# Inverse transform matrices from sines instead of TensorE turns, a new opening and a new order in a long-convolution and FFN kernel

## The chip, the cores and the metric

The kernel runs on one core of one Trainium2 chip. The metric is the device time of one execution in microseconds (us). The engines are called as in the profile: PE is TensorE (PEld its weight loads), DVE is VectorE, ACT is ScalarE, POOL is GpSimd, SP is the engine whose queue issues most DMAs.

## The reference

All tensors are bf16; S = 2048 rows, D = 640 columns, F = 1728. The input x is normalized, goes through a gated convolution (A) and through a two-layer FFN (B), and the two are multiplied and added to x.

```
xn = layernorm(x)
# A: shift filter of 4 taps on k, gate by v, causal convolution of length S per column, gate by xn
k_shift = sum over t of k[s - (3 - t)] * shift_k[:, 3 - t]
kv = k_shift * v
y = irfft(rfft(kv padded to 2S) * rfft(ssm_k padded to 2S))[:S] + kv * ssm_D
s = xn * y
# B
g = silu(gelu(xn @ w1 + b1) @ w2 + b2)
out = x + s * g
```

## The kernel before

The convolution is computed as a Fourier transform of 4096 points in two steps, written as matrix products. The rows are split as 128 partitions times NJ = 16. A first product (F1) takes the 16 groups of 128 rows through 128x128 matrices that hold cosines and sines, for the filter (steps `kf`, evictions `ke`) and for kv (`uf`, `ue`). The results go to DRAM (`ks`, `us`) and come back with the rows regrouped (`fl`, `ml`). A second product (F2, `ff` and `mu`) uses small 32x32 blocks. The two transforms are multiplied (`mp`, `mq` on DVE: the second factor has real and imaginary rows exchanged by the DMAs `mk`), a first inverse product follows (`ma`, `mb`, eviction `me`), a trip through DRAM again (`ms`, `yl`), and the second inverse product `y`. `yt` multiplies by the gate, `yo` adds x, `ys` stores. Each 1280-column pair of rows is cut into three tiles of 428, 426 and 426 columns, one PSUM bank each, so there are 48 tiles in each of these steps and 24 in `y`.

The FFN works on four chunks of 512 rows. `h` is a tile of the first product (14 per chunk: h0 to h13, h14 to h27, h28 to h41, h42 to h55), `he` its GELU on ACT, `g` a tile of the second product (8 per chunk, 14 matmuls of 320 columns each), `ge` its SiLU on ACT, `gm` the multiplication into xn on DVE. Layernorm of the chunks 1 to 3 is `ls` (statistics, DVE), `lv`, `lr` (the root, POOL), `ln` (normalization, DVE or ACT), `tt` and `te` (turn and eviction). `kt` and `kc` turn the filter. `cv` are the eight DVE steps of the shift filter for each of eight pairs of rows.

The cosine and sine matrices of F1 are WA and WB, 128 x 16 x 128 each. They are made once, from an integer product of row and column numbers (`build_f1_product`, `w`), by Sin and Abs on ACT (`ws`). The second inverse product needs the same matrices, each 128x128 block turned; GA and GB are the names for these, in the same memory. Before, 32 turns on PE (`it`, four steps of eight) and four DVE copies (`ie`) turn WA and WB in place once F1 is done with them.

Everything is issued in one hand-ordered list: after `prologue()` the string `PLAN` names step after step, and its letters behind a dot say which engine evicts (`.a` ACT, `.d` DVE). Each engine works through its own instructions in that order. PSUM banks and slots of the working area are handed out from lists in the order of the plan (`ones`, `slots`). `TURNS` says for each tile which rotation of the 32x32 blocks it uses. `use_table` keeps count of which set of functions ACT has loaded: GELU with one, SiLU with another, and Sin runs with the second.

The opening, `prologue()`, loads x, w1 and the parameters, runs warming products (`warm`, products of the identity whose result nobody reads), takes the four taps of the shift filter over the partitions (`tap`), normalizes chunk 0 in two halves (`bn`, `ag`, `sq`, `rc`, `norm_dve`), turns them (`turn`, `turned_out`) and does the first six FFN1 tiles in two halves (`first_block`). The bias b1 and the skip weight D arrive as rows (`prm`), are turned on PE into the bank `pt` and copied by DVE. `small_bits`, `small_first` and `small_second` prepare the small matrices of F2 and of the first inverse.

Of the kernel before, what the change touches and what calls it, by code (L numbers as in the profile page):

```python
# [10 lines left out]
F32 = mybir.dt.float32  # L11
BF16 = mybir.dt.bfloat16
I32 = mybir.dt.int32
ACT = mybir.ActivationFunctionType
# [14 lines left out]
WARM = (6, 3, 1)  # L29
NFIRST = 6  # L30

TURNS = "301213011202320033233310212313130220012202211303"

PLAN = """
em4 s h13 he1 em7 w he0 X1 ls5 K1 K0 he3 he5 he2 ls6 ls7 ls4 lv1 lr1 em6 em5 h12 h9 he13 he4 h10 ee7.a he12 ee6.a
ee5.a he9 ee4.a h11 cv8 cv16 cv17 ln5.d B1 B0 he10 h6 cv0 cv18 cv19 ln4.d h7 ln7.a he11 ln6.a h8 tt9 cv9 cv1 he6 B2
he7 tt8 tt5 C4 he8 ss g0 ws0 ge0 cv10 cv20 cv21 te8.d tt6 g2 g1 tt7 C0 C3 C1 cv22 cv11 cv2 te9.d te6.d cv12 sm C2
te7.d X2 d K3 V6 cv3 kt9 kc9.d kt7 ws1 te5.a ws2 kt5 V0 K2 ge1 kc7.a ge2 cv4 gm1.d V3 V1 V5 kc5.d kt3 kt13 kt14 kf28
kc14.a kt11 kt2 kt8 ke28.a kc3.d kc11.d V2 kc8.a kt10 kt12 kc13.d kc2.d kc10.d kt6 kf10 kt4 V4 kc12.a X3 V7 ke10.a
kf15 kf27 kc4.d kc6.d kf9 kt1 kc1.d kt15 ke27.a ke15.a kf31 kt0 kc15.d kc0.d ke9.a kf41 cv32 cv33 cv5 gm0.d ke31.a  # L40
kf16 kf39 kf17 ke16.a kf44 kf11 kf29 kf45 kf14 ke17.a ke11.a ke29.a ke44.a ke45.a ke39.a ke41.a ks9 ks3 g3 ge3 kf38
kf42 kf24 ke42.a cv34 ke14.d cv6 cv13 cv7 cv14 cv40 kf13 kf33 kf12 kf40 ke24.a kf0 ke33.a ke13.a gm3.d cv35 ke40.a kf3
ke12.a ke3.a g4 ke0.a gm2.d ge4 kf30 kf34 ke34.a kf46 kf37 kf35 ke30.a kf5 kf47 g5 ks4 ke46.a ke47.a ks13 cv36 cv37
ke38.a ke5.a ke37.a ks15 ke35.a kf36 ke36.a cv24 cv38 ks11 kf4 kf32 ke4.a kf6 kf1 kf21 kf43 ke21.a ke6.a ke32.a ge5
ke43.a g6 ks5 ks1 ks12 cv48 cv39 cv56 cv49 cv41 cv23 ge6 kf2 ke2.a cv57 cv42 cv43 gm4.d kf23 kf25 kf22 kf20 kf26
ke23.a ke22.a cv50 ke25.a g7 uf26 ke1.a cv51 cv15 ke20.a ke26.a ue26.a ks14 ks10 kf18 uf4 ue4.a kf19 ke19.a ke18.a
uf14 kf8 uf24 kf7 ue24.a h26 ks0 ks7 ks8 ks6 ue14.a ke8.a ke7.a ks2 ge7 gm7.d uf25 h15 uf12 ue25.a ue12.a uf13 ue13.a
he26 h20 h24 uf0 ue0.a he15 he24 uf27 uf8 h21 fl15 uf5 he20 he21 h19 he19 ue8.a uf9 uf17 ue17.a h22 he22 ue5.a ue9.a
uf16 uf28 ue27.a ue28.a ls8 cv44 cv45 cv52 cv46 gm6.d cv47 ls10 ue16.d cv25 h23 uf10 uf33 he23 h16 us8 uf29 ue33.a
ue29.a uf32 uf34 ue32.a uf15 uf35 h27 he16 ue35.a h18 he27 uf3 h25 he18 ue10.a us4 cv53 gm5.d ue3.a ue15.a he25 cv26  # L50
uf7 h17 he17 ls11 cv27 cv54 fl1 fl11 fl7 fl9 fl14 ls9 cv28 cv55 ue7.d lv2 cv29 cv58 us5 fl5 fl2 uf6 ue6.a ue34.a lr2
cv59 h14 uf40 uf1 uf2 uf11 uf38 uf30 fl4 fl3 he14 uf37 ue2.a ue11.a ue1.a g8 ue30.a ue38.a ge8 uf31 uf41 ln8.d cv60 g9
cv30 cv61 ue40.a ue41.a fl0 fl6 fl8 ue31.a cv31 uf22 uf39 uf23 ue22.a ue23.a uf21 uf19 uf36 ue21.a ue39.a ge9 ln9.d
cv62 ln10.d cv63 ue19.a ue37.a g10 uf18 ff10 ls12 ue36.d ln11.d fl12 ff46 ff13 ff8 ge10 ue18.a uf20 uf45 fe10.d uf42
uf44 uf43 us11 us2 us9 us0 us3 us10 us1 ue20.d fe8.a ue45.a ue44.a fe13.a ff15 ff7 ff19 uf46 ue42.d uf47 ue43.d fe46.a
tt13 fe19.d ff23 ff21 fe15.d ff6 ff3 ue46.a ue47.a fe7.a us13 us7 te13.d us12 fe21.d fe23.a ff2 us6 tt12 tt10 fe3.a
fe6.d it2 ff24 ff12 ff4 tt14 us14 te10.a fe2.a te12.d ie2.d te14.d it0 us15 fe12.a fe4.a fe24.a mk2 tt11 ff47 ff11
ff36 ie0.d te11.d fl10 it1 fe11.a fe36.a ls14 ie1.d gm8.d ff9 ff16 ff1 ff28 fe1.a fe28.a fe9.a ml2 g11 fe47.a fe16.a
ff29 ff38 ff44 ls15 fe38.d ge11 ff25 ff33 ff27 it3 fe44.a ml3 ff20 ff14 ff26 fe29.a fe27.a fe25.a fe26.a fe33.a fe14.a
ml0 ml4 mk3 ml1 ml8 g12 ff35 mu7 ff18 gm9.d ie3.d ls13 mu6 fe20.d gm11.d ff5 mu8 ff34 gm10.d lv3 ge12 g14 fe18.a  # L60
fe34.a mp7 mp8 mq8 mu9 ma7 lr3 fe35.a fe5.a mu10 mq7 ff43 mk4 ml7 mk1 ff42 fe42.a mb7 g13 mp6 mp9 mq6 mp10 mq10 ln15.a
fe43.a me7.a ge13 ff22 mu13 gm12.d mq9 ff0 ff17 mu11 fe0.a fe22.a ge14 fe17.a ln12.a mp11 mq11 g15 mu12 mp13 mq13
gm13.d ge15 mk8 mu24 ff30 h39 mp12 mq12 mp24 ff32 ff45 mu26 mu4 h28 fe30.a he39 fe45.a he28 fe32.a mp4 mp26 mq24 mq4
mq26 h29 mu5 mu14 he29 ma11 mb11 ff37 ff31 ma24 h30 fe37.a fe31.a mk6 me11.a ml6 fl13 mp5 mq5 ma5 ma9 mu25 ma10 mb24
mp14 mq14 he30 mb5 mp25 mq25 mu19 ml11 mb9 ml5 mb10 mk5 me24.a h40 mu18 ma6 ma8 me9.a mu2 me10.a me5.a he40 mp19 mq19
mb8 ff41 fe41.a me8.a h32 ma12 ma13 mu16 mb13 mk0 mp18 mb12 mp2 mq18 mp16 mq16 mb6 h34 mu3 he32 ma4 ff40 me13.a me6.a
me12.a mq2 mp3 mk7 he34 mu22 mb4 mu15 ff39 fe39.a mp15 mp22 h31 me4.a fe40.a he31 h36 ma14 q6 ml9 mq22 mq3 mq15 mu21
# [798 lines left out]
```

## Time and profile before

| | us |
|---|---|
| median of 3 runs | 200.44 |
| lowest and highest | 200.13, 200.51 |
| the profiled execution | 202.52 |
| its span, first to last instruction | 200.7 |
| granted clock, mean | 0.991 |

| engine | busy us | share |
|---|---|---|
| PE | 189.0 | 94% |
| DVE | 171.8 | 86% |
| ACT | 154.7 | 77% |
| POOL | 43.5 | 22% |

The profile is one execution; its busy times are the union of instruction durations, and durations of neighbours on one engine overlap a little. An "idle before" in brackets names the length of the wait and what ended it. The windows view gives, for a stretch of the span, the busy time of each engine, then the clock that TensorE was granted (1.00 is full), then the share of the DMA engines and their rate in GB/s.

### The profile page before, as it was taken

Reading aid. Unit: us, or ns where it says so; the run is one execution under the profiler, and the core shown is the slowest. Engines: PE = TensorE matmul, PEld = TensorE weight load, DVE = VectorE, ACT = ScalarE, POOL = GpSimd, SP = SyncE. Lnnn points to the kernel's source line nnn. Section 1 sums busy time; section 2 is a strip of 40 time slices with the busy share of each in tenths; the row PEclk is TensorE's granted clock in tenths of the full one; section 3 lists DMA queues with packets and bytes.
Section 4 is the critical chain, followed back from the end, with each engine's and each line's share of the span. In section 5 each row is a group of like instructions: output and inputs, shape, how many; then the busy total and the mean of one; then the engine's idle time right before and its main releaser. Section 6 shows DMA issues by size and latency. Waiting matters only on the chain.

```text
span 200.7 us, 5123 instructions
## 1 busy us (share of the span) xinstructions
PE 189.0 (94%) x1941; PEld 113.3 (56%) x1954; DVE 171.8 (86%) x366; ACT 154.7 (77%) x311; POOL 43.5 (22%) x77
## 2 busy tenths in 40 slices
PE   7699999799999999999999999997999999999990
PEld 2377467776665455656656334454665544677770
DVE  7769999999999999989999999999899500479991
ACT  3546999999999999999989999996877538801120
POOL 8100400003454003753020000113145500001230
PEclk9969999999999999999999999999999999999999
DMA  6999999983598899799899978989469869951164
GB/s 200 346 365 308 338 394 409 399 319 137 219 366 322 284 350 364 291 341 344 266 314 337 283 242 280 331 286 349 139 229 330 289 212 369 395 219 65 50 251 163
DMA packets 27057, 57.69 MB, mean 287 GB/s; under 512 B 3032, under 2 KB 15513, under 8 KB 27032
## 3 DMA queue, kind: packets, MB, share of 16 engines
q1 hardware_dynamic: 22528, 39.65, 57.4%
q0 software_dynamic: 4320, 17.70, 23.8%
q8 instruction: 15, 0.25, 0.5%
q14 instruction: 10, 0.08, 0.1%
q10 hardware_dynamic: 184, 0.01, 0.1%
HBM read 33.76 MB, written 18.35 MB: 260 GB/s over the span
## 4 chain that ended last, share of the span: by engine, by line
PE 52%; ACT 34%; DVE 5%; issue 3%; DMA 3%; POOL 1%; ACTq 1%; POOLq 0%
PE banks L486 22%; ACT area L145 19%; PE banks L460 13%; PE banks L409 6%; ACT hT L472 5%; DMA prm<-in_A_ssm_D_dram 3%; ACT sl L492 2%; PE banks L742 2%; PE banks L675 2%; PE banks L676 2%; DVE st L416 2%; PE banks L444 1%; ACT xn L435 1%; DVE area L630 1%; ACT WA L322 1%
## 5 line engine op out<-in xcount | busy, mean ns | idle before, releaser
L145 ACT CAST area<-banks 128x426 bf16<-128x426 f32 (+2 forms) x179 | 81.7, 639 | 3.9 <-PE banks L409 3.6
L486 PE MATMUL banks<-w_sb,hT 128*128 128x320 bf16 x448 | 65.6, 299 | 0.3
L460 PE MATMUL banks<-xnT,w_sb 128*128 128x512 bf16 x217 | 53.6, 379 | 0.7
L486 PEld LDWEIGHTS <-hT 128*128 128x128 bf16 x448 | 42.9, 98 | 20.0 <-issue 3.0
L630 DVE TENSOR_TENSOR area<-banks,area 128x426 bf16<-128x426 f32 (+1 forms) x96 | 50.4, 595 | 1.9 <-PE banks L409 1.1
L472 ACT ACTIVATE hT<-banks,b_f 128x512 bf16<-128x512 f32 x52 | 34.2, 705 | 7.0 <-PE banks L460 5.2
L460 PEld LDWEIGHTS <-w_sb 128*128 128x128 bf16 x230 | 21.4, 98 | 25.9 <-issue 3.9
L492 ACT ACTIVATE sl<-banks 128x320 bf16<-128x320 f32 x32 | 15.4, 493 | 20.6 <-PE banks L486 14.5
L570 DVE TENSOR_TENSOR area<-area 128x1280 bf16<-128x1280 bf16 x32 | 25.4, 818 | 0.3
L684 DVE TENSOR_TENSOR area<-banks,xn 128x426 bf16<-128x426 f32 (+1 forms) x18 | 10.0, 596 | 15.5 <-PE banks L676 15.5
L660 POOL DMA_DIRECT2D scrC<-area x16 | 11.7, 731 | 44.1 <-DVE area L630 25.0
L409 PE MATMUL banks<-area,mats 32*32 32x426 bf16 (+1 forms) x768 | 19.4, 345 | 0.1
L566 DVE TENSOR_TENSOR area<-area 128x1280 bf16<-128x1280 bf16 x24 | 19.3, 814 | 0.0
L526 PE MATMUL banks<-area,WB 128*128 128x214 bf16 (+1 forms) x64 | 15.6, 299 | 0.1
L526 PE MATMUL banks<-area,WA 128*128 128x212 bf16 (+1 forms) x64 | 15.3, 298 | 0.1
L541 POOL DMA_DIRECT2D scrK<-area x16 | 8.8, 554 | 30.2 <-ACT area L145 29.1
L409 PEld LDWEIGHTS <-mats 32*32 32x32 bf16 x768 | 8.0, 88 | 11.1 <-issue 8.6
L552 POOL DMA_DIRECT2D scrU<-area x16 | 8.7, 546 | 18.7 <-ACT area L145 17.2
L146 DVE CAST area<-banks 128x426 bf16<-128x426 f32 (+1 forms) x17 | 9.5, 590 | 1.7 <-ACT area L145 1.1
L498 DVE TENSOR_TENSOR xn<-xn,sl 128x320 bf16<-128x320 bf16 x32 | 9.9, 318 | 1.0 <-ACT sl L492 1.0
L416 DVE BATCH_NORM_STATS2 st<-xn 128x6 f32<-128x320 bf16 x24 | 10.4, 476 | 0.0
L693 POOL DMA_DIRECT2D out_dram<-area x6 | 3.3, 547 | 31.9 <-DVE area L689 26.4
(101 smaller groups left out, 194.6 us busy)
## 6 DMA issues: line engine op xcount, KB each, us to landing
scrK<-area POOLq DMA_DIRECT2D x16, 320.0 KB, 3.0
scrU<-area POOLq DMA_DIRECT2D x16, 320.0 KB, 3.6
area<-scrK SPq DMA_DIRECT2D x16, 320.0 KB, 7.1
area<-area SPq DMA_DIRECT2D x32, 160.0 KB, 3.6
area<-scrU SPq DMA_DIRECT2D x16, 320.0 KB, 5.3
scrC<-area POOLq DMA_DIRECT2D x16, 320.0 KB, 4.0
area<-scrC SPq DMA_DIRECT2D x16, 320.0 KB, 6.5
area<-in_A_k_dram SPq DMA_DIRECT2D x4, 640.0 KB, 9.4
```

What stands on the lines that cost most here:

```text
L145: return nc.scalar.copy(out=out_ap, in_=in_ap)
L409: nc.tensor.matmul(out=out[b, :], lhsT=mats[a, m, a], rhs=rhs[a, :], start=start, stop=stop)
L416: nc.vector.bn_stats(out=st[:, j, h, :], in_=xn_tiles[c][:, j, h * HALF:(h + 1) * HALF])
L460: nc.tensor.matmul(out=ps, lhsT=w1_sb[:, t, ft * P:(ft + 1) * P], rhs=xnT[:, t, :], start=(t == 0), stop=(t == DT - 1))
L472: nc.scalar.activation(out=hT[:, ft, :], in_=one(("h", i)), func=ACT.Gelu_apprx_tanh, bias=b1_f[:, ft:ft + 1], scale=1.0)
L486: nc.tensor.matmul(out=ps[:, 0:HALF], lhsT=hT[0:M, ft, q * P:(q + 1) * P], rhs=w2_sb[0:M, ft, hs], start=(ft == 0), stop=(ft == FT - 1))
L492: nc.scalar.activation(out=sl[:], in_=one(("g", i))[:, 0:HALF], func=ACT.Silu)
L526: nc.tensor.matmul(out=ps[:, dst], lhsT=(WA, WB)[r][:, n2, :], rhs=rows[:, n2 % 2, src], start=True, stop=True)
L566: nc.vector.tensor_tensor(out=uc, in0=uc, in1=tmp, op=ALU.add)
L570: nc.vector.tensor_tensor(out=tmp if s else uc, in0=kh[:, r0:r0 + KC, :], in1=w_exp[:, j:j + 1, :].to_broadcast([P, KC, D]), op=ALU.mult)
L630: nc.vector.tensor_tensor(out=flat(("p", i))[:, x * w:x * w + w], in0=one(("mu", i))[:, 0:w], in1=flat(key)[:, cols(j)], op=ALU.mult)
L660: nc.gpsimd.dma_start(out=pair_view(scrC)[g2], in_=pair(("c", g2)))
```

## The change

Three parts of the code change, and with them the whole order.

The inverse matrices are computed directly. `ir` makes on POOL two short integer vectors per partition; for each quarter i of 4 x 128 columns, `ip` makes on DVE the integer product that stands in the turned matrix, `ia` takes it modulo L, `is` makes the sine on ACT into GB, `ib` the absolute value, and `ic` the cosine into GA. The integers lie in a slot of the working area. `it` and `ie` are gone. In the new order quarter 1 stands around the last products of the filter and kv, and the quarters 2, 3 and 0 around and after the last FFN1 tiles, the sines of quarter 0 and 3 directly after the last GELU.

In the opening, the turn of the parameters moves from before the turn of x to between two of the first FFN1 tiles; four warming products instead of one precede the turn of x, and three new ones follow it; the integer bits for the small matrices are made in three places instead of one.

The mean times root of the layernorm (`lb`) becomes one DVE instruction instead of two on POOL.

The order names the same steps otherwise, on new places, and some evictions change engine: ten instead of seven `fe`, two instead of one `ke`, seven instead of six `ue`, nine instead of eight `te` go to DVE, and 11 instead of 12 `kc`, two instead of three `me`. `TURNS` has a new string.

```
-WARM = (6, 3, 1)
+WARM = (6, 3, 4, 3)
...
     def ln_root(c):
         rstd = take(("rs", c), small, [P, CH], F32, "rstd")
         nc.gpsimd.tensor_tensor(out=rstd[:], in0=live["ve", c][:], in1=mhalf[:, 0:CH], op=ALU.pow)
+
+    def ln_bias(c):
         nb = take(("nb", c), small, [P, CH], F32, "nb")
-        nc.gpsimd.tensor_tensor(out=nb[:], in0=live["mv", c][:, :, 0], in1=rstd[:], op=ALU.mult)
-        nc.gpsimd.tensor_scalar(out=nb[:], in0=nb[:], scalar1=-1.0, scalar2=None, op0=ALU.mult)
+        nc.vector.scalar_tensor_tensor(out=nb[:], in0=live["mv", c][:, :, 0], scalar=-1.0, in1=live["rs", c][:],
+                                       op0=ALU.mult, op1=ALU.mult)
...
-    def i2_tr(i):
-        tp = one_bf(("it", i))
-        for q in range(8):
-            nc.tensor.transpose(out=tp[:, q * P:(q + 1) * P], in_=(WA, WB)[i // 2][:, i % 2 * 8 + q, :], identity=ident[:])
-
-    def i2_out(i, eng):
-        q4 = i % 2
-        evac(eng, (GA, GB)[i // 2][:, q4 * 8:(q4 + 1) * 8, :].rearrange("p a b -> p (a b)"), one_bf(("it", i)))
-        ones.drop(("it", i))
+    def i2_rows():
+        nc.gpsimd.iota(kcol[:], pattern=[[0, 1]], base=1, channel_multiplier=2, allow_small_or_imprecise_dtypes=True)
+        for t, n in ((kn, P), (kj, NJ)):
+            nc.gpsimd.iota(t[:], pattern=[[1, n]], base=0, channel_multiplier=0)
+            nc.gpsimd.tensor_scalar(out=t[:], in0=t[:], scalar1=kcol[:], scalar2=None, op0=ALU.mult)
+
+    def i2_index(i, dtype):
+        return flat(("w", i))[:, 0:4 * P * 2].bitcast(dtype).rearrange("p (a b) -> p a b", a=4)
+
+    def i2_product(i):
+        nc.vector.scalar_tensor_tensor(out=i2_index(i, I32), in0=kn[:, None, :].to_broadcast([P, 4, P]), scalar=float(NJ),
+                                       in1=kj[:, 4 * i:4 * i + 4, None].to_broadcast([P, 4, P]), op0=ALU.mult, op1=ALU.add)
+
+    def i2_phase(i):
+        nc.vector.tensor_single_scalar(out=i2_index(i, I32), in_=i2_index(i, I32), scalar=L - 1, op=ALU.bitwise_and)
+
+    def i2_sine(i):
+        use_table("sine")
+        nc.scalar.activation(out=GB[:, 4 * i:4 * i + 4, :], in_=i2_index(i, I32), func=ACT.Sin,
+                             scale=(2.0 * math.pi / L) * (1.0 - SIN_EPS), bias=sin_bias[:])
+
+    def i2_abs(i):
+        nc.scalar.activation(out=i2_index(i, F32), in_=i2_index(i, I32), func=ACT.Abs, scale=1.0, bias=half_l[:])
+
+    def i2_cosine(i):
+        use_table("sine")
+        nc.scalar.activation(out=GA[:, 4 * i:4 * i + 4, :], in_=i2_index(i, F32), func=ACT.Sin,
+                             scale=2.0 * math.pi / L, bias=sin_bias_h[:])
+        slots.drop(("w", i))
...
         pt = banks[:, 5, :].bitcast(BF16)
-        nc.tensor.transpose(out=pt[:, 0:FT + DT], in_=prm[:, :], identity=ident[0:FT + DT, 0:FT + DT])
         warm(WARM[2])
...
-        small_bits()
+        small_bits(30)
...
         turn(0)
         turn(1)
+        warm(WARM[3], 5)
         bn(2, 0)
         turned_out("d", 0, 0)
         turned_out("a", 1, 0)
         bn(2, 1)
         ag(2)
-        nc.vector.tensor_copy(out=b1_f[:], in_=pt[:, 0:FT])
-        nc.vector.tensor_copy(out=dD_sb[:], in_=pt[:, FT:FT + DT])
         bn(3, 0)
         bn(3, 1)
         ag(3)
+        small_bits(1)
         for i in range(NFIRST - 1):
             first_block(0, i)
-        small_first()
+            if i == 1:
+                nc.tensor.transpose(out=pt[:, 0:FT + DT], in_=prm[:, :], identity=ident[0:FT + DT, 0:FT + DT])
+        nc.vector.tensor_copy(out=b1_f[:], in_=pt[:, 0:FT])
         sq(2)
         rc(2)
         norm_dve(2)
         norm_dve(3)
+        nc.vector.tensor_copy(out=dD_sb[:], in_=pt[:, FT:FT + DT])
+        small_bits(96)
+        small_first()
         small_second()
```

The new order, around the first use of the inverse matrices (the other lines of `PLAN` are left out):

```
+mu45 g22 me39.a me31.a me47.a ms4 me43.a me32.a ms6 ms13 ma35 gm19.d mp33 mq33 mp45 mq45 ma33 ma22 ip1 ia1 ma30 mb35
+mb33 mb22 ge22 mb30 mu42 mu44 mu46 me22.a me35.a me33.a me30.a ms7 is1 ib1 h43 h53 h50 mp42 mp46 mp44 mq42 mq44 mq46
...
+he50 h49 h55 he49 he48 h44 he46 h52 he43 he52 h51 he44 he51 he55 h54 ms14 gm22.d h45 ms15 yl5 he53 he54 he45 h47 yl7
+yl6 y11 y9 y10 ip2 he47 g24 yl12 yl4 q1 yl1 yl2 ip3 ip0 ia2 yt11 ia0 ia3 yl0 is0 ib0 is3 ib3 ic0 y7 yt10 yt7 yt9 yo3.d
+ge23 g25 ge24 ge25 y6 y2 yt2 gm23.d y8 y0 y1 yt0 yt1 yl11 ic3 y18 yt6 yt8 yt18 yo2.d yo0.d is2 ib2 ic2 y3 g27 y17 yl9
```

119 lines of the change are left out of this document (59 added, 60 removed).

## The prediction

> **What bounds the kernel now.** I read the page first, then the busy time by stage, then the timeline of the opening and of the tail.
>
> ```profile
> span 200.7 us, 5123 instructions
> ...
> PE 189.0 (94%) x1941; PEld 113.3 (56%) x1954; DVE 171.8 (86%) x366; ACT 154.7 (77%) x311; POOL 43.5 (22%) x77
> ...
> DVE  7769999999999999989999999999899500479991
> ```
>
> PE looks like the bound with 94%, but DVE's row of slices has no digit under 8 from the fourth to the 31st, and then a hole. So I cut the span into stages: from the end of the opening to about the last F1 matmul, on to the last product, the third FFN1 behind it, and the inverse F1 with the last FFN2. Columns are the length, the busy time of PE, PEld, DVE, ACT and POOL, then clock and DMA.
>
> ```profile
> 15.24:91.30 76.06, 74.41 (x560) 47.61 (x563) 74.22 (x141) 73.98 (x151) 20.65 (x36) 1.00 0.90 324
> 91.30:156.40 65.10, 62.88 (x1028) 34.53 (x1034) 63.00 (x134) 58.26 (x124) 11.88 (x19) 1.00 0.85 286
> 156.40:172.30 15.90, 15.79 (x115) 7.62 (x115) 1.83 (x4) 9.88 (x17) 2.56 (x4) 1.00 0.83 296
> 172.30:196.00 23.70, 23.67 (x175) 16.61 (x173) 21.04 (x47) 5.55 (x11) 3.26 (x6) 1.00 0.49 186
> ```
>
> In the first stage DVE is idle for 76.06 - 74.22 = 1.84 us and ACT for 2.08. In the second DVE is idle for 2.10, ACT for 6.84. In the third DVE works 1.83 of 15.90 and PE all of it; in the fourth PE works 23.67 of 23.70. PE's busy time counts overlapping latencies, so its 62.88 of 65.10 is not full use. I read: DVE (with ACT) sets the time up to 156.4, PE from there to 196.
>
> **The opening.** The granted clock is the column behind POOL's.
>
> ```profile
> 7.00:8.00 1.00, 0.04 (x1) 0.07 (x1) 0.99 (x3) 1.00 (x2) 0.00 (x0) 1.00 1.07 375
> ...
> 9.00:10.00 1.00, 0.37 (x5) 0.34 (x5) 0.96 (x3) 0.58 (x1) 0.00 (x0) 0.97 1.05 365
> 10.00:11.00 1.00, 1.00 (x7) 0.74 (x5) 1.00 (x5) 0.00 (x0) 0.00 (x0) 0.50 1.11 405
> ...
> 13.00:14.00 1.00, 1.00 (x9) 0.83 (x8) 0.22 (x1) 0.12 (x1) 0.00 (x0) 0.83 1.09 373
> ```
>
> ```profile
> 4.66 1.46 PE L724 MATMUL banks<-ident 128*128 128x512 bf16 x3
> 6.06 0.92 PE L601 MATMUL banks<-skT,ident 4*128 4x320 bf16 x4
> 7.96 0.17 PE L774 MATMUL banks<-ident,prm 19*128 19x19 bf16 x1 [0.98 <-DMA prm<-in_A_ssm_D_dram]
> 8.06 0.39 PE L724 MATMUL banks<-ident 128*128 128x512 bf16 x1
> 8.28 0.72 PE L733 MATMUL banks<-ident,xn 128*128 128x128 bf16 x10
> 8.93 0.56 DVE L146 COPY xnT<-banks 128x768 bf16<-128x768 bf16 x1 [0.94 <-PE banks L733]
> 9.63 4.55 PE L742 MATMUL banks<-xnT,w_sb 128*128 128x256 bf16 x25 [0.63 <-ACT xnT L145]
> 11.84 0.80 DVE L716 TENSOR_SCALAR xn<-xn,mv,rstd 128x640 bf16<-128x640 bf16 x2
> 14.59 4.14 PE L742 MATMUL banks<-xnT,w_sb 128*128 128x256 bf16 x35
> 14.68 0.56 DVE L146 COPY xnT<-banks 128x768 bf16<-128x768 bf16 x1 [1.45 <-PE banks L733]
> ```
>
> PE waits at 7.96 for the parameters' DMA, then for xnT to 9.63; after these near-empty stretches its clock is 0.50 from about 9.9 to 13.3, and 25 products take 4.55 us where 35 later take 4.14 (0.118 each). DVE has had the second pair of rows normalized since 12.64 and waits 1.45 for PE. With the change the parameters' turn no longer holds up PE, four warming products of 0.22 (8.28 - 8.06) follow the taps (6.98), so the turn starts at 7.85 instead of 8.28, three more fill the wait for xnT, and the 25 products take 2.9, from about 9.2 to 12.1: before DVE's normalization is done. The 1.45 goes; the 0.94 shrinks by the turn's 0.43 but grows by the bits moved out from in front of it; the rest of DVE's work in the opening is the same, only reordered. Upper bound of the gain 1.45, and I count 1.2 on paper. Lower bound: if the clock falls all the same, nothing, and minus 0.4 if the four products run at 0.4 to 0.5 each, as the three at 4.66 did. I take -0.9, because DMA is at 1.05 to 1.11 in these rows and the loads come no sooner.
>
> In a sentence of its own: the Trainium skill (TensorE: Matmul & The Clock Gate, Part 1) says that the clock is gated by windows of about 3.4 us that run free of the kernel, and that their place differs from run to run. The 3.4 us between 9.9 and 13.3 agree; by that rule the -0.9 would hold in some executions and be another number in others, which is one of the rivals below.
>
> **The inverse matrices.** Prices:
>
> ```profile
> 93.44 0.61 PE L590 MATMUL banks<-ident,WB 128*128 128x128 bf16 x8
> ...
> L146 DVE COPY WB<-banks 128x1024 bf16<-128x1024 bf16 x2 | 1.4, 692 | 0.0
> L146 DVE COPY WA<-banks 128x1024 bf16<-128x1024 bf16 x2 | 1.3, 668 | 0.1
> ...
> L299 DVE TENSOR_TENSOR area<-area 128x2048 int32<-128x2048 f32 x1 | 2.3, 2293 | 0.6 <-POOL area L298 0.6
> ...
> L351 DVE SCALAR_TENSOR_TENSOR area<-area 128x128 f32<-128x128 f32 x2 | 0.7, 345 | 0.0
> ...
> L303 DVE TENSOR_SCALAR area<-area 128x2048 int32<-128x2048 int32 x1 | 1.2, 1221 | 0.0
> ...
> L380 DVE TENSOR_SCALAR area<-area 128x384 int32<-128x384 int32 x1 | 0.4, 362 | 0.0
> ...
> L317 ACT ACTIVATE WB<-area,sin_bias 128x2048 bf16<-128x2048 int32 x1 | 2.0, 1987 | 0.0
> ...
> L385 ACT ACTIVATE area<-area,sin_bias 128x384 f32<-128x384 int32 x1 | 0.6, 601 | 0.0
> ```
>
> Removed: 32 turns on PE, four groups of at most 0.61 (2.0 to 2.4 in all), and four DVE copies, 2 x 0.692 + 2 x 0.668 = 2.72, all in the second stage. Added per quarter of 512: a DVE product, by the line between L351 and L299 (1.015 ns an element) 0.345 + 384 x 1.015 = 0.73 (bounds 0.45, if 16-bit inputs run at twice the rate, and 1.1); a bit mask, by L380 and L303 0.43; three ACT passes, by L385 and L317 (0.833 ns) 0.71 each, 0.62 back to back. Only quarter 1 stands before the last product in the order (1.16 on DVE; its ACT passes meet an ACT with 6.84 idle). Quarters 0, 2 and 3 stand in the third stage, where DVE has 14 us idle: nothing, unless a product is later than y11. No table load is added: seven changes of set before, seven after, by the order's own text.
>
> **Moved evictions and the root.**
>
> ```profile
> L146 DVE CAST area<-banks 128x426 bf16<-128x426 f32 x10 | 5.8, 592 | 1.7 <-ACT area L145 1.1 <-PE banks L409 0.6
> ...
> L146 DVE COPY xnT<-banks 128x512 bf16<-128x512 bf16 x8 | 3.3, 417 | 0.0
> ...
> L146 DVE COPY area<-banks 128x640 bf16<-128x640 bf16 x12 | 5.1, 485 | 0.1
> ```
>
> Counting the suffixes of both orders up to the last product, DVE gets three more K evictions (fe), one ke and one ue (5 x 0.59), one te (0.42), and loses one kc (0.485): +2.9. The three mean-times-root steps, on 4 columns, cost DVE between nothing and the 0.345 that L351 takes on 128; I take 0.2: +0.6. In front of each stand other DVE steps while POOL makes the root, so no wait for it is counted; if that cover is gone, the steps queued behind it on DVE (the copies and products that feed PE) wait as long as POOL does. What ACT gains, an earlier bias for its normalization, hides behind its GELUs. DVE up to its last product: -2.72 + 1.16 + 2.9 + 0.6 = +1.9 by durations, and since overlapping instructions issue some 0.06 apart from their durations (six more of them) I take +1.7.
>
> POOL, 22% busy, gets five small index steps (ir) in place of six; ahead of them in its queue stands only the last root, behind them the first store of the inverse, which waits for ACT anyway: nothing. In sentences of their own: the Trainium skill (GPSIMD Engine Reference, Specifications) says that POOL shares its SBUF interfaces with VectorE and contends with instructions that have two SBUF inputs. By that rule some tenths would be added; no row quoted here shows such a stall, and the products that stand beside ir read one side from PSUM.
>
> **The stage in the middle.** DVE's idle 2.10 us there is what can absorb the added work.
>
> ```profile
> 143.19 5.20 DVE L630 TENSOR_TENSOR area<-banks,area 128x428 bf16<-128x428 f32 x10 [0.93 <-PE banks L409]
> ```
>
> The largest single gap in it, 0.93, is a wait for PE, and PE has 2 us less to do before it. I take half of the 2.10 as gone, -1.05 (bounds 0 and -2.1, and above nothing if the new order has new gaps).
>
> **The tail.**
>
> ```profile
> 160.29 7.72 PE L460 MATMUL banks<-xnT,w_sb 128*128 128x512 bf16 x34
> 170.17 3.23 ACT L472 ACTIVATE hT<-banks,b_f 128x512 bf16<-128x512 f32 x5
> 173.42 1.28 ACT L492 ACT_TABLE_LOAD   x1
> 173.67 0.34 PE L675 MATMUL banks<-area,WA 128*128 128x426 bf16 x1
> 173.85 0.34 PE L676 MATMUL banks<-area,WB 128*128 128x426 bf16 x1
> 188.18 7.78 PE L486 MATMUL banks<-w_sb,hT 128*128 128x320 bf16 x56
> ```
>
> An FFN1 tile is 5 x 0.222 = 1.1 us, an FFN2 tile 7.78 / 4 = 1.94, a y tile 2 x 0.18 = 0.36. The old order has two tiles of the third FFN1 (h50, h53) ahead of the last product, the new one three (h43, h53, h50), so PE has 1.1 less behind it: -1.1. Behind the last FFN1 tile (172.3 in the old clock) PE does y11, y9, y10, g24, y7, g25, y6 = 4 x 0.36 + 2 x 1.94 + 0.36 = 5.7, until 178.0, and then wants y2, which needs both sines of quarter 0. ACT ends the last GELU at 173.4, loads its table (1.28, then a touch of 0.2), and does five passes at 0.62: 178.0, just in time. Then three SiLUs and the third quarter's cosine end at 179.7, and y18 could start at 179.4. For these two I add 0.35 (bounds 0 and 1.2). The end itself, SiLU, product, add and store, is the same.
>
> Sum: -0.9 + 1.7 - 1.05 - 1.1 + 0.35 = -1.0. The profiled execution took 202.52 us with its 200.7 span, against a median of 200.44 (200.13 to 200.51), so I take the difference off the median: 200.44 - 1.0 = 199.4.
>
> **Rivals.** First, PE is the bound all the way from 91, as its 94% suggests: then all of DVE's added work hides in its gaps (-2.1 instead of -1.05) and the tail's waits vanish: 200.44 - 0.9 + 1.7 - 2.1 - 1.1 = 198.0. For it: hardly a gap in PE. Against: DVE's 63.00 of 65.10. Second, slower: DVE is the bound to the last product and its gaps stay or grow by half a microsecond, while ACT, with 6.84 idle, is given less. Then the load costs 1.7 and the gaps 0.5, and the opening and the third tile give the same as above: 200.44 + 2.2 - 0.9 - 1.1 + 0.35 = 201.0. It decides, against no change, once DVE's idle between the last F1 eviction and the last product comes to about 2.1 us again. Third, ACT's five passes end 1.2 later than 178.0: PE stands for the whole of it, 200.6. Fourth, the opening does not do what it says, the clock still falls to 0.50: 200.3, or 200.7 with slow warming products.
>
> **How the numbers follow.** Forecast 0.36 (own range 198.8 to 200.0), first rival 0.18, second 0.24, third 0.10, fourth 0.12. The range takes the first rival whole, and most of the second: 198.0 to 201.4. About 0.2% is what a measurement can tell here (the three runs spread by 0.19%). Faster by more: the first rival, most of the forecast and a little of the rest, 0.54; within it 0.16, mostly from the third and fourth; slower 0.30, the second and the bad ends of the others.
>
> **What would show it.** Right: clock 1.00 from 10 to 13, xnT's second copy near 13.5; the last product about 0.3 us earlier; three FFN1 tiles before it; PE without a gap over 0.4 after the last FFN1 tile. Wrong: a clock of 0.50 in the opening, DVE idle above 2.1 between 91 and its last product, ACT's cosine of quarter 0 ending after PE reached y2, or index products well over 0.73.

## The result and the profile after

| | before | after |
|---|---|---|
| median (22 runs of each, side by side) | 201.83 us | 199.72 us |
| lowest and highest | 200.13, 203.51 | 199.25, 201.47 |
| ratio after / before, 95% interval | | 0.9923 [0.9893, 0.9952] |
| profiled execution, its span | 202.52, 200.7 | 201.46, 199.6 |

The changed kernel is faster, by 1.0 to 2.2 us by the interval. The ratio compares means and leaves out three slow runs of the kernel before, above 203.1; the medians differ by 2.11. The 200.44 from which the forecast started lies near the quick end of the 22 runs of the kernel before.

The page of the kernel after: its span, the busy times, and DVE's row of slices. DVE's hole ahead of the tail is shorter, since the index work of three quarters stands in it.

```profile
span 199.6 us, 5103 instructions
...
PE 189.8 (95%) x1916; PEld 111.6 (56%) x1928; DVE 175.0 (88%) x377; ACT 162.3 (81%) x320; POOL 43.0 (22%) x76
...
DVE  7499998999999999989999999999899930389992
```

**One mark makes executions comparable.** Up to the start of DVE's second copy of 128x768 into xnT, at the end of the opening, executions differ by some microseconds; behind it they are much more alike. So each kernel is described by when its first and second copy start and by three lengths behind the second copy: to the end of the last product (`mp`, `mq`), from there to the end of the last FFN1 tile, from there to the end of DVE's last addition, and on to the end of the span. The sum of all from the second copy on is called the rest. The span is printed to a tenth, so the last length and the rest are good to 0.05.

| us | 1st copy | 2nd copy | to last product | to last FFN1 tile | to last addition | to the end | rest |
|---|---|---|---|---|---|---|---|
| before | 8.93 | 14.68 | 141.70 | 16.00 | 24.77 | 3.55 | 186.02 |
| after | 10.00 | 14.76 | 142.16 | 14.19 | 25.57 | 2.92 | 184.84 |
| difference | +1.07 | +0.08 | +0.46 | -1.81 | +0.80 | -0.63 | -1.18 |

There is one trace of each kernel. How well the mark repeats can be seen from pairs with one order and two openings: to the last product they differ by 0.01 to 0.05 in three pairs, but by 0.44 in the fourth, the two kernels with turns further down, where in the later one DVE waits 0.36 for a DMA among the products. A difference under about 0.4 up to the last product is therefore not shown by a single pair of traces.

In these two executions the whole gain, 202.52 - 201.46 = 1.06, lies behind the opening. The windows view between the second copy and the end of the last product (length, then busy time of PE, PEld, DVE, ACT, POOL, clock, DMA), first of before, then of after:

```profile
14.68:91.30 76.62, 74.97 (x566) 48.01 (x568) 74.78 (x142) 74.43 (x151) 20.65 (x36) 1.00 0.90 323
91.30:156.38 65.08, 62.86 (x1028) 34.53 (x1034) 62.98 (x134) 58.26 (x124) 11.86 (x19) 1.00 0.85 286
```

```profile
14.76:91.38 76.62, 74.53 (x554) 47.49 (x556) 74.37 (x144) 74.18 (x148) 18.39 (x30) 1.00 0.87 318
91.38:156.92 65.54, 63.48 (x1018) 33.36 (x1016) 64.07 (x139) 59.38 (x124) 14.61 (x24) 1.00 0.83 279
```

DVE's busy time goes from 74.78 + 62.98 = 137.76 to 138.44, its idle time from 141.70 - 137.76 = 3.94 to 3.72. So +0.68 of work and -0.22 of waiting make the +0.46. Of the waiting, 0.41 came in the first window and 0.63 went in the second.

Groups of after, with the prices of what was added (busy, mean ns of one, idle before):

```profile
L602 DVE SCALAR_TENSOR_TENSOR area<-kn,kj 128x512 int32<-128x512 int16 x4 | 2.6, 684 | 0.0
L606 DVE TENSOR_SCALAR area<-area 128x512 int32<-128x512 int32 x4 | 1.6, 420 | 0.0
...
L432 DVE SCALAR_TENSOR_TENSOR nb<-mv,rs 128x4 f32<-128x4 f32 x3 | 0.5, 151 | 0.0
```

The timeline of after at the tail. 176.87 and 178.45 are the weight loads of y2 and y18: both wait for cosines.

```profile
173.38 0.71 ACT L610 ACTIVATE WB<-area,sin_bias 128x512 bf16<-128x512 int32 x1
...
176.11 0.71 ACT L618 ACTIVATE WA<-area,sin_bias_h 128x512 bf16<-128x512 f32 x1
176.72 1.07 ACT L497 ACTIVATE sl<-banks 128x320 bf16<-128x320 f32 x3
176.87 0.10 PEld L700 LDWEIGHTS <-WA 128*128 128x128 bf16 x1 [0.55 <-ACT WA L618]
177.67 0.73 ACT L618 ACTIVATE WA<-area,sin_bias_h 128x512 bf16<-128x512 f32 x1
...
178.45 0.10 PEld L700 LDWEIGHTS <-WA 128*128 128x128 bf16 x1 [0.21 <-ACT WA L618]
```

### The profile page after: what moved, and what is told of

It is laid out like the page before. It is cut to its first block, busy times and chain, and to the rows that moved or that the text cites. A ratio compares the mean times of both kernels' runs of the same rounds, so it can differ in the third digit from the quotient of the medians.

```text
span 199.6 us, 5103 instructions
## 1 busy us (share of the span) xinstructions
PE 189.8 (95%) x1916; PEld 111.6 (56%) x1928; DVE 175.0 (88%) x377; ACT 162.3 (81%) x320; POOL 43.0 (22%) x76
## 4 chain that ended last, share of the span: by engine, by line
PE 76%; ACT 16%; DVE 4%; issue 2%; POOL 0%; POOLq 0%; ACTq 0%
PE banks L491 26%; PE banks L465 21%; PE banks L412 7%; ACT area L147 7%; PE banks L531 6%; ACT hT L477 4%; PE banks L749 3%; PE banks L520 2%; PE banks L700 2%; PE banks L449 2%; PE banks L701 2%; PE banks L767 2%; ACT sl L497 2%; PE banks L461 1%; PE banks L626 1%
## 5 line engine op out<-in xcount | busy, mean ns | idle before, releaser
L147 ACT CAST area<-banks 128x426 bf16<-128x426 f32 (+2 forms) x175 | 80.7, 627 | 3.9 <-PE banks L412 3.4
L465 PE MATMUL banks<-xnT,w_sb 128*128 128x512 bf16 x218 | 52.8, 379 | 0.7
L477 ACT ACTIVATE hT<-banks,b_f 128x512 bf16<-128x512 f32 x52 | 35.4, 719 | 5.1 <-PE banks L465 3.0
L497 ACT ACTIVATE sl<-banks 128x320 bf16<-128x320 f32 x32 | 14.8, 491 | 14.5 <-PE banks L491 13.2
L412 PE MATMUL banks<-area,mats 32*32 32x426 bf16 (+1 forms) x768 | 20.6, 345 | 0.6 <-DVE area L148 0.2
L148 DVE CAST area<-banks 128x426 bf16<-128x426 f32 (+1 forms) x21 | 11.4, 592 | 1.7 <-PE banks L412 0.7
L428 POOL TENSOR_TENSOR rs<-ve,mhalf 128x4 f32<-128x4 f32 x3 | 4.1, 1352 | 32.1 <-DVE ve L424 32.1
```

The source lines that it names most:

```text
L147: return nc.scalar.copy(out=out_ap, in_=in_ap)
L148: return nc.vector.tensor_copy(out=out_ap, in_=in_ap)
L412: nc.tensor.matmul(out=out[b, :], lhsT=mats[a, m, a], rhs=rhs[a, :], start=start, stop=stop)
L465: nc.tensor.matmul(out=ps, lhsT=w1_sb[:, t, ft * P:(ft + 1) * P], rhs=xnT[:, t, :], start=(t == 0), stop=(t == DT - 1))
L477: nc.scalar.activation(out=hT[:, ft, :], in_=one(("h", i)), func=ACT.Gelu_apprx_tanh, bias=b1_f[:, ft:ft + 1], scale=1.0)
L497: nc.scalar.activation(out=sl[:], in_=one(("g", i))[:, 0:HALF], func=ACT.Silu)
```

## The experiments

Twelve kernels ran. The theory at the start was the prediction's: the opening, one FFN1 tile more ahead of the last product, and sines that cost DVE less than turned copies, which paid for evictions moved to DVE. Its rivals were that the order alone, or the sines alone, made the gain, and that only DVE, or only PE, sets the time. Lengths come from each kernel's profiled execution, and "the rest" is the one defined above.

### The opening, taken back and done alone

One kernel is the changed one with the old opening, the other the kernel before with the new opening:

```
-WARM = (6, 3, 4, 3)
+WARM = (6, 3, 1)
...
+        nc.tensor.transpose(out=pt[:, 0:FT + DT], in_=prm[:, :], identity=ident[0:FT + DT, 0:FT + DT])
         warm(WARM[2])
...
-            if i == 1:
-                nc.tensor.transpose(out=pt[:, 0:FT + DT], in_=prm[:, :], identity=ident[0:FT + DT, 0:FT + DT])
```

> The changed kernel with the opening of before (six, three and one warming products, the parameters' turn ahead of the turn of x, the bits in one place); sines and order stay. Theory of the prediction (the opening gives about 0.9 us, DVE's later last product and one FFN1 tile more ahead of it the rest): 0.9 us above the changed kernel, a ratio to before of 0.996 to 0.997. Rival 'the opening is nearly all of it, through the clock': 1.5 us or more above the changed kernel, a ratio of 0.999 to 1.001, and as wide a spread as before's. Rival 'PE is the bound and the 2 us of turns are the gain': within 0.3 us of the changed kernel, a ratio of 0.992 to 0.994.

> The kernel before with the new opening alone; turns on TensorE, root on POOL and order as before. Theory of the prediction: 0.9 us below before, ratio 0.995 to 0.996. Rival 'the opening is nearly all of it': 1.5 us below, ratio 0.992 to 0.993, and a narrower spread than before's. Rival 'the turns are the gain': ratio 0.998 to 1.000.

| us | 1st copy | 2nd copy | between | rest | median |
|---|---|---|---|---|---|
| before, old opening | 8.93 | 14.68 | 5.75 | 186.02 | 201.62 |
| before with the new one | 8.21 | 12.97 | 4.76 | 186.03 | 200.92, ratio 0.9985 [0.9947, 1.0022] |
| after with the old one | 8.21 | 13.74 | 5.53 | 184.86 | 200.39, ratio 0.9959 [0.9923, 0.9995] |
| after, new opening | 10.00 | 14.76 | 4.76 | 184.84 | 199.72, ratio 0.9923 [0.9893, 0.9952] |

The rests stay with the order (186.0 and 184.9), so opening and rest add up. The opening is worth 0.67 to 0.70 by the medians. By the ratios it is 0.7 in the changed kernel, with intervals that overlap, and only 0.3 in the kernel before, whose 0.9985 has no change in its interval, misses the expected 0.995 to 0.996 and has the number of the rival that sees the gain in the turns. So the whole times alone do not show the opening's gain; the traces do. Between the copies the old one took 5.53, 5.75, 5.75 and 5.77 in the four profiled kernels that have it, the new one 4.76 or 4.77 in all ten: a gain of 0.77 to 1.01. What varies more is the first copy, 7.83 to 10.00 with the new opening and 8.17 to 10.62 with the old. The timeline of after, and then of before with the new opening, shows why:

```profile
7.22 1.89 PE L749 MATMUL banks<-ident 128*128 128x512 bf16 x4
8.90 1.27 PE L758 MATMUL banks<-ident,xn 128*128 128x128 bf16 x10
10.00 0.56 DVE L148 COPY xnT<-banks 128x768 bf16<-128x768 bf16 x1 [2.19 <-PE banks L758]
...
14.76 0.55 DVE L148 COPY xnT<-banks 128x768 bf16<-128x768 bf16 x1
```

```profile
6.69 1.04 PE L722 MATMUL banks<-ident 128*128 128x512 bf16 x4
7.56 0.72 PE L731 MATMUL banks<-ident,xn 128*128 128x128 bf16 x10
8.21 0.56 DVE L146 COPY xnT<-banks 128x768 bf16<-128x768 bf16 x1 [0.41 <-PE banks L731]
...
12.97 0.55 DVE L146 COPY xnT<-banks 128x768 bf16<-128x768 bf16 x1
```

The same four warming products take 1.89 in one and 1.04 in the other, and the turn 1.27 and 0.72: PE still ran at half its rate up to about 10.6 in the first. The windows view prints 1.00 there only because the trace has no record of the clock yet; the first one stands at 10.63 in after and at 5.97 in the other. Neither second copy waits for PE; DVE works through between the copies, and that is the constant 4.76. In the old opening the second copy always waited (1.45 before, 1.24 in after with the old opening), and in all four traces that have it the granted clock falls to 0.50 inside the opening, as at 9.93 to 13.35 before and 8.52 to 11.93 in after with the old opening. In the ten traces with the new opening no record of 0.50 stands ahead of 195 us. In the windows view of after the clock, the third number from the end, is full where before had 0.50:

```profile
11.00:12.00 1.00, 1.00 (x11) 0.83 (x9) 0.96 (x4) 0.00 (x0) 0.00 (x0) 1.00 1.01 410
12.00:13.00 1.00, 1.00 (x10) 0.78 (x9) 0.89 (x6) 0.75 (x2) 0.00 (x0) 1.00 1.00 406
```

The fall of the clock and the wait of the second copy go together in all fourteen traces; that the clock makes the wait, and so the 0.8 to 1.0, is argued from this. Which part of the new opening keeps the clock up, the moved turn of the parameters or the three products behind the turn of x, no run separates; four warming products are not needed for it, as two kernels with one show further down.

The Trainium skill (TensorE: Matmul & The Clock Gate, Part 1) lets the gate's windows run free of the kernel. The differing place of the first record and of the falls agrees with that; the other part of what I drew from it, that the gain itself would differ, does not, since it is 0.8 to 1.0 in every pair.

### Sines or turns: the new order with turns, the old order with sines

The changed kernel with `it` and `ie` put back at the places of the old order, and without the index steps; that with the old opening too; and the kernel before with sines instead of turns, quarter 1 ahead of the last products, the others ahead of the third FFN1's GELUs:

```
 ... fe31.a us12
+it2
 gm9.d ln11.d
+ie2.d it0
 g11 ge11
+ie0.d
 ...
-ip1 ia1  ...  -is1 ib1  ...  -ic1  ...  -ip2  ...
```

> The changed kernel with the inverse matrices turned on PE again and copied by DVE (four groups between us12 and ls13), no sines at the end; opening, root and order stay. Theory of the prediction: DVE gets 2.7 us back in the middle and loses 1.2 ahead of its last product, which then comes 0.5 to 1.3 us later; the waits for the cosines in the tail (0.35 to 0.85 us) go; so within 0.5 us of the changed kernel, ratio to before 0.990 to 0.995. Rival 'PE is the bound and the turns are the gain': 1.8 to 2.4 us above the changed kernel, ratio 1.001 to 1.004. In the trace: y2 no longer waits for ACT.

> The new order and the root on DVE alone: opening of before, turns on PE as in the run with turns. Theory of the prediction: opening 0.9 above, so a ratio of 0.996 to 0.999. Rival 'the opening is nearly all of it': 0.999 to 1.001. Rival 'the turns are the gain': 1.002 to 1.005, since then the new order without the sines brings nothing.

> The kernel before with the sines alone: no turns on PE, no copies; quarter 1 beside the last products, the other quarters' DVE steps behind them and all their ACT passes ahead of the third FFN1's GELUs; opening, root on POOL and the rest of the order as before. Counted from DVE's second copy of xnT in the opening to the end of the span, before takes 186.02 us and the changed kernel 184.84. Theory 'DVE is the bound to its last product': DVE does 2.7 less and 1.1 more ahead of it, so the last product comes 1.3 to 1.6 earlier, the GELUs a little later: 184.5 to 185.0. Rival 'PE is the bound': the 2.0 to 2.4 us of turns go at once: 183.6 to 184.1. Rival 'the sines are worth something only in the new order': 185.7 or more.

| us | to last product | DVE busy in it | DVE idle in it | rest | ratio to before |
|---|---|---|---|---|---|
| before | 141.70 | 137.76 | 3.94 | 186.02 | |
| after | 142.16 | 138.44 | 3.72 | 184.84 | 0.9923 [0.9893, 0.9952] |
| new order with turns | 145.18 | 139.97 | 5.21 | 187.51 | 1.0082 [1.0042, 1.0122] |
| that with the old opening | 145.62 | 139.87 | 5.75 | 187.91 | 1.0089 [1.0047, 1.0131] |
| old order with sines | 142.46 | 136.28 | 6.18 | 190.38 | 1.0265 [1.0193, 1.0336] |

The new order with turns is slower than the old one by 3.5 up to the last product (3.9 with the old opening, where the trace is of the longest of its twelve executions, 206.13 us), so the order is no gain by itself (it was not made for turns, which the number includes). My expectation, turns worth under 0.5, fell; with 2.67 more of rest than after, the rival that sees the gain in their removal is nearest, and exceeded (its ratios were 1.001 to 1.004 and, with the old opening, 1.002 to 1.005). But the old order with sines is not faster either: DVE has 1.48 less to do and 2.24 more to wait. My expectation of 184.5 to 185.0 fell as well, and so did the rival of 183.6 to 184.1. (Its rest of 190.38 holds 3.6 of another kind: 12 ACT passes ahead of the GELUs, which then start at 167.47, and the last FFN1 tile ends 19.59 behind the last product instead of 16.00.) Neither half gains; only both together do.

Why shows in stretches of ten microseconds, 70 to 80 and 80 to 90 behind the second copy. The kernel before, the old order with sines, the changed kernel, then the new order with turns; the third column of busy times is DVE, the fourth ACT:

```profile
84.68:94.68 10.00, 9.71 (x124) 5.73 (x123) 9.16 (x20) 10.00 (x26) 4.30 (x8) 1.00 0.92 343
94.68:104.68 10.00, 9.87 (x163) 6.46 (x161) 9.62 (x26) 9.81 (x24) 1.47 (x3) 1.00 0.93 289
```

```profile
83.92:93.92 10.00, 9.65 (x122) 5.58 (x121) 8.76 (x20) 10.00 (x26) 4.32 (x8) 1.00 0.90 343
93.92:103.92 10.00, 9.63 (x135) 5.11 (x134) 7.85 (x23) 9.74 (x24) 2.35 (x6) 1.00 0.94 313
```

```profile
84.76:94.76 10.00, 9.48 (x121) 5.06 (x118) 9.43 (x19) 9.99 (x24) 5.80 (x11) 1.00 0.86 326
94.76:104.76 10.00, 9.82 (x166) 5.87 (x158) 9.65 (x27) 9.96 (x25) 1.30 (x3) 1.00 0.81 273
```

```profile
82.59:92.59 10.00, 9.47 (x120) 5.06 (x118) 9.44 (x19) 9.99 (x24) 5.74 (x11) 1.00 0.86 327
92.59:102.59 10.00, 8.76 (x153) 5.86 (x138) 9.89 (x25) 8.19 (x20) 0.00 (x0) 1.00 0.79 271
```

ACT has no time left before the change either, with 10.00 and 9.81 of 10. With the turns' copies gone from the old order, it is at 10.00 and 9.74 and DVE starves at 8.76 and 7.85. With the copies put back into the new order, DVE is at 9.89 and ACT at 8.19 in the second stretch. The changed kernel has both above 9.4 in both.

### Six evictions back on ACT

The direct test of that reading: `fe25`, `fe2`, `fe16`, `ue30`, `ke2` and `te10` of the changed kernel go from DVE to ACT.

```
-fe25.d fe2.d fe16.d  ...  ue30.d  ...  ke2.d  ...  te10.d
+fe25.a fe2.a fe16.a  ...  ue30.a  ...  ke2.a  ...  te10.a
```

> The changed kernel with six evictions (three fe, one ue, one ke, one te) given back from DVE to ACT, 3.4 us less work on DVE and as much more on ACT. If DVE alone sets the time up to the last product: that product at 139.0 to 140.5 behind the opening's second copy of xnT (142.16 in the changed kernel), and 182 to 183.5 to the end of the span (184.84). If ACT's evictions set the pace just where the turned copies stood, so that the copies' time is worth something only as evictions moved to DVE: the last product at 142.2 to 144.5, and 184.8 to 187 to the end.

The last product came at 144.69, the rest is 187.45, the median 202.14, ratio 1.0062 [1.0022, 1.0102]. The same stretches of its windows:

```profile
83.05:93.05 10.00, 9.59 (x107) 5.45 (x106) 7.73 (x16) 9.97 (x24) 6.18 (x12) 1.00 0.79 299
93.05:103.05 10.00, 9.39 (x134) 5.11 (x130) 8.29 (x23) 10.00 (x25) 0.27 (x1) 1.00 0.78 278
```

DVE's work up to the last product falls from 138.44 to 135.95 and its waiting grows from 3.72 to 8.74. So 2.5 us less on DVE make the kernel 2.6 slower. In this stretch ACT sets the pace, and what I had booked as a cost of 2.9, evictions moved to DVE, is where the gain is made. What the sines pay for is room on DVE for them. No run put load on ACT alone; that ACT is the limit here rests on this run and on its full rows.

### Load on DVE, load on PE

Three additions of 512 elements on DVE, whose result nobody reads, spread between the third layernorm's statistics and the last products; and ten products of 512 columns on PE in two places:

```
+    def idle_dve(i):
+        nc.vector.tensor_tensor(out=one(("zd", i)), in0=w1_sb[:, 0, 0:512], in1=w1_sb[:, 1, 0:512], op=ALU.add)
...
+    def idle_pe(i):
+        for _ in range(5):
+            nc.tensor.matmul(out=ps.rearrange("p (a b) -> p a b", a=4), lhsT=ident[:],
```

> The changed kernel with three more DVE additions of 512 columns (about 0.53 us each, 1.6 in all) among the products, whose results nobody reads. From the second copy of xnT to the end (changed kernel: 184.84): theory 'DVE is the bound to its last product' 186.0 to 186.5; rival 'PE is the bound', 184.8 to 185.3.

> The changed kernel with ten more PE products of 512 columns (about 0.216 us each, 2.2 in all) in two places among the products, whose results nobody reads. From the second copy of xnT to the end (changed kernel: 184.84): theory 'DVE is the bound to its last product' 184.8 to 185.5; rival 'PE is the bound', 186.5 to 187.0.

With the additions the last product came at 143.85 (+1.69), the rest is 186.60 (+1.76), the median 201.15; with the products 144.40 (+2.24), 187.15 (+2.31), 202.45. Both loads pass through whole. DVE's waits among the products, in the timeline of the kernel with more PE products:

```profile
102.27 3.15 DVE L665 TENSOR_TENSOR area<-banks,area 128x426 bf16<-128x426 f32 x6 [0.96 <-PE banks L412]
121.15 13.33 DVE L665 TENSOR_TENSOR area<-banks,area 128x426 bf16<-128x426 f32 x26 [1.17 <-issue]
142.78 1.11 DVE L665 TENSOR_TENSOR area<-banks,area 128x428 bf16<-128x428 f32 x2 [1.00 <-PE banks L412]
```

The first two waits are new (2.13 together, about the products' own time; for the second the profile names no releaser), the third was 0.89 in after:

```profile
142.55 1.11 DVE L655 TENSOR_TENSOR area<-banks,area 128x428 bf16<-128x428 f32 x2 [0.89 <-PE banks L412]
```

"DVE alone is the bound", which wanted the products hidden, fell, and so did "PE alone", which wanted the additions hidden. In this order, at these places, a microsecond added to either engine is a microsecond of the kernel.

### The tail, and a version that beats both

First a kernel with one warming product instead of four ahead of the turn of x, quarter 0's cosine ahead of quarter 3's sine, and the unread mean times root of chunk 2 left out:

```
-WARM = (6, 3, 4, 3)
+WARM = (6, 3, 1, 3)
...
-is0 ib0 is3 ib3 ic0
+is0 ib0 ic0 is3 ib3
```

> The changed kernel with one warming product instead of four ahead of the turn of x, the cosine of quarter 0 ahead of quarter 3's sine, and without the root step of chunk 2, which nothing reads. Theory: the wait of 0.47 us for y2 goes and DVE saves 0.15, so 184.2 to 184.5 from the second copy of xnT to the end; the second copy itself comes 0.3 to 0.7 sooner than in the changed kernel at the same clock; median 0.6 to 1.0 us below the changed kernel's 199.7, ratio to before 0.987 to 0.989. Rival 'the four warming products are what lifts the clock': with one, the clock falls as in the old opening, second copies between 12.2 and 16.4, and the median is no better than the changed kernel's.

The clock does not fall in its opening and the second copy starts at 12.75, so the four warming products are not what holds the clock, though the median that this rival named, no better than after's, came in. Its rest is 185.25, 0.41 worse than after, the median 199.68, ratio 0.9904 [0.9875, 0.9932], which overlaps that of after; my theory fell. Of the 0.41, 0.20 stands ahead of the last product (142.36), within what the mark leaves open, and 0.16 in the tail. There y2's wait went, but y18 waited in its place:

```profile
176.63 0.72 ACT L610 ACTIVATE WB<-area,sin_bias 128x512 bf16<-128x512 int32 x1
176.80 0.10 PEld L700 LDWEIGHTS <-WA 128*128 128x128 bf16 x1 [0.66 <-ACT WA L618]
```

Swapping two quarters moves the wait, since ACT has the same six passes behind the table load. So the next kernel takes quarter 0's five steps out of there, to where ACT already has the sine's table:

```
+ip0 ia0                     (behind mq46)
 ma44 ms10 ... me46.a me44.a ic1
+is0 ib0 ic0
 me45.d me42.d ...
-ip0 ia0 is0 ib0 ic0         (behind y10)
```

> The changed kernel with quarter 0's product, mask and three ACT passes moved ahead of the last GELUs, so that ACT has both its sines before y2. Measured from the start of the opening's second copy of xnT to the end of the span (184.84 in the changed kernel). My theory, that the tail lost about 0.45 us to the waits for the cosines of quarters 0 and 3: both waits go, the last product stays at 142.16 behind the copy, 184.3 to 184.5. Rival: ACT is the tighter engine ahead of the GELUs, so that 2 us more of its work there start the GELUs later and PE waits for a bank or for hT: 184.8 or more, with the end of the last FFN1 tile later than 14.19 behind the last product.

Both waits are gone. The last product stays at 142.16, the last FFN1 tile at 14.19 behind it, the last addition 25.14 behind that instead of 25.57. The rest is 184.60, 0.1 above what I expected, because the end took 3.11 instead of 2.92. The median is 198.98 (4 runs), ratio 0.9892 [0.9836, 0.9949]. The timeline:

```profile
172.71 0.72 ACT L618 ACTIVATE WA<-area,sin_bias_h 128x512 bf16<-128x512 f32 x1
...
174.24 0.34 PE L701 MATMUL banks<-area,WB 128*128 128x428 bf16 x1
174.42 0.34 PE L700 MATMUL banks<-area,WA 128*128 128x426 bf16 x1
...
175.86 0.34 PE L700 MATMUL banks<-area,WA 128*128 128x428 bf16 x1
```

The row at 172.71 is the cosine of quarter 3, done at 173.43. y2 begins at 174.42, right behind y6's last product, and y18 at 175.86. Last, that kernel with one warming product instead of four:

> The changed kernel with two edits: quarter 0's product, mask and three ACT passes ahead of the last GELUs (as in the experiment on the tail alone, which gave 184.60 from the start of the opening's second copy of xnT to the end), and one warming product instead of four ahead of the turn of x. The first is worth 0.24 from that copy to the end, so 184.6 again. If the warming products only shift the start of the turn within the chip's clock, the copy starts in the profiled execution somewhere from 12.6 to 14.8 as in the executions with four, and the median is 198.9 to 199.5; if one instead of four is enough and takes 0.65 (three of 0.22) off the way to the turn whatever the clock does, the copy starts at or below 12.5 and the median is 198.3 to 198.9; if the four are what keeps the clock up, the copy starts at 13.7 or later, as with the old opening, and the median is 200.0 or more.

First copy 7.84, second 12.61, rest 184.39, median 198.80 (198.75 to 200.34, 6 runs), ratio 0.9886 [0.9834, 0.9938]: the lowest of all, though its interval overlaps those of after and of the kernel before this one. The copy at 12.61 lies in the range of the first reading, that the number of warming products matters little; the median lies in that of the second, 198.3 to 198.9, though 0.18 below the kernel with four is no difference that these runs can tell. The third reading fell. The timeline says why one product can't save time once the clock is up: the turn waits for DVE's normalization and begins at 7.10, where with four products it began at 7.11.

```profile
5.88 0.39 PE L749 MATMUL banks<-ident 128*128 128x512 bf16 x1
6.60 0.80 DVE L741 TENSOR_SCALAR xn<-xn,mv,rstd 128x640 bf16<-128x640 bf16 x2
7.10 0.81 PE L758 MATMUL banks<-ident,xn 128*128 128x128 bf16 x10 [0.84 <-DVE xn L741]
```

### The mean times root back on POOL

```
-        nc.vector.scalar_tensor_tensor(out=nb[:], in0=live["mv", c][:, :, 0], scalar=-1.0, in1=live["rs", c][:], ...)
+        nc.gpsimd.tensor_tensor(out=nb[:], in0=live["mv", c][:, :, 0], in1=live["rs", c][:], op=ALU.mult)
+        nc.gpsimd.tensor_scalar(out=nb[:], in0=nb[:], scalar1=-1.0, scalar2=None, op0=ALU.mult)
```

> The changed kernel with the mean times root on POOL again, two instructions a chunk. My theory counted the DVE step at 0.2 us, three times, hidden by nothing: the last product 0.3 to 0.6 earlier than 142.16 behind the opening's second copy of xnT. Rival: POOL's longer chain makes ACT's or DVE's normalization wait for it, by 0.3 or more in a chunk, and the last product stays or comes later, up to 143.

The last product came at 142.39, 0.23 later, and the rest is 185.09, 0.25 longer; the median is 200.08, ratio 0.9946 [0.9902, 0.9989]. My theory fell: DVE without its three steps is not earlier. Up to 95.4 behind the second copy the two kernels agree to 0.02, with all three steps passed, so on DVE they cost nothing that shows; the difference arises among the products of the 24 us behind it, where DVE's 47 take 24.57 instead of 24.34. A jump of 0.44 among these products also separates the two kernels with turns, whose order is one, so this 0.2 need not come from POOL; its mechanism is open.

## Why the prediction was right

The forecast was 199.4 with a range of 198.0 to 201.4, and the median is 199.72. The change it forecast, -1.0, stands against 1.0 to 2.2 by the interval and 2.11 by the medians: the way is right, the size is at the small end. That 199.4 lies so near 199.72 is in part luck, since it starts from 200.44, 1.4 below the later median of 201.83. Behind the second copy the terms came to -1.18 instead of -0.1, as +0.46 and -1.01 against +0.65 and -0.75, and 0.63 at the end that the forecast did not have. By its own steps:

- **What bounds.** "DVE (with ACT) up to 156.4" holds for the pair. Counting only DVE's work was wrong: between 70 and 90 us behind the second copy it is ACT that has no time left, before the change (10.00 and 9.81 of 10) as after it.
- **The opening, -0.9.** Right in mechanism and size: 0.77 to 1.01 between the copies, the clock no longer falls to 0.50, and the second copy's 1.45 wait is gone; the medians have 0.67 to 0.70, within their noise. In the profiled execution itself the lower bound came true (four warming products at 0.43, the turn at 8.90 instead of the 7.85 forecast), and the gain of that part was eaten there by the later start.
- **The index steps.** The product was 0.68 (forecast 0.73), the mask 0.42 (0.43), an ACT pass 0.72 (0.71).
- **DVE's work, +1.7.** Measured +0.68 of busy time. The named steps were counted rightly: by durations they come to +1.70 instead of +1.9, with five more evictions of the 0.59 kind (14 and 19 ahead of the last product) and the root at 0.15 a time instead of 0.2. But the instructions that both kernels have are together 0.67 shorter, why is open, and the overlap of neighbours takes 0.35 instead of 0.2.
- **DVE's waits, -1.05.** Mis-sized: -0.22 up to the last product. In the middle stage, which the term is about, the waiting fell by 0.63, but 0.41 more came ahead of it. The gap of 0.93 for PE (`mp` behind the third layernorm) is still there with 0.89, although PE lost its turns. The two errors nearly cancel: +0.65 forecast, +0.46 measured.
- **POOL's index steps, nothing.** They ran from 104.47 to 106.06; beside them DVE's six products took 3.15 (0.525 each), the seven behind them 3.69 (0.527). The Trainium skill (GPSIMD Engine Reference, Specifications) states contention for DVE instructions with two SBUF inputs; these read one side from PSUM, so they do not test it.
- **The tail.** One FFN1 tile more stands ahead of the last product, five products of 0.222 as forecast; its 1.1 is part of the -1.81. The tile y11, 0.36, moved behind the last FFN1 tile and is in both differences, -1.81 and +0.80. The waits for the cosines came to 0.43, as the last experiments on the tail showed (forecast 0.35). Up to the last addition -1.81 + 0.80 = -1.01 stands against -0.75.
- **"The end itself is the same."** Wrong: 0.63 shorter, the largest term that I did not have. All kernels with the new order end 2.9 to 3.1 behind the last addition, those with the old one 3.5 to 3.6. In the timeline of before, three of POOL's stores go out beside SP's last ones, in that of after only one, at 192.87. That these are what takes longer is argued, not shown; no run moved a store alone.

The timeline of before, then of after, at the end:

```profile
191.48 6.04 SPq L510 DMA_DIRECT2D out_dram<-xn  x5
193.22 1.07 POOL L693 DMA_DIRECT2D out_dram<-area  x2 [3.10 <-DVE area L689]
194.69 0.54 POOL L693 DMA_DIRECT2D out_dram<-area  x1 [0.41 <-DVE area L689]
```

```profile
192.87 0.54 POOL L718 DMA_DIRECT2D out_dram<-area  x1 [1.30 <-DVE xn L503]
193.31 3.74 SPq L515 DMA_DIRECT2D out_dram<-xn  x5
```

The first rival (PE the bound) and the second (DVE the bound) both supposed one engine. The load runs leave neither. The third, PE held by ACT's passes, came in small, 0.43 instead of 1.2. The fourth, a clock that still falls to 0.50, did not come true; only its slow warming products did, in the profiled execution, because PE had not reached its full rate yet. Of the signs named in advance, the clock held and the three FFN1 tiles stood where they should. But the last product ended 0.5 later in the two profiled executions (156.92 and 156.38) instead of 0.3 earlier, and one sign of being wrong was there: the cosine of quarter 0 ended at 176.82, after PE had waited 0.55 for it.

## What to carry to other kernels

A step that takes work off an engine with short waits is worth what that engine's suppliers allow: take the load in stretches of ten microseconds, see which of the two engines is at 10.0 of 10, and book a moved eviction as a gain where the receiving engine would have waited. Do the halves of a change alone before crediting either: here sines without the order gained nothing, and the order without sines lost 3.5 up to the last product. And measure executions from a mark behind the opening, so that its spread of microseconds does not hide the rest; differences of a few tenths need more than one pair of traces even so.

## What of the hardware was unexpected

In the opening PE ran at half rate until 4.09 us in one execution and until 10.63 in another with the same first products: 512-column products take about 0.43 each there and 0.22 later. The trace's record of the granted clock begins only where PE gets its full rate, between 4.09 and 6.60 in the thirteen other traces, and the windows view prints 1.00 ahead of it. In nine of the ten traces with the new opening this came before the warming products ahead of the turn of x began, so their number, one or four, did not decide it. Behind the opening kernels repeat well, but not always: the last product ends 141.69 to 141.70 behind the second copy in two kernels with the old order and 142.11 to 142.16 in four with the new one, but 145.18 and 145.62 in the two with turns.
